# Spectral layer and feed-forward network on one core: even and odd frequencies apart in two of the four DFT stages

## The chip, the cores and the metric

The kernel runs on one core of one Trainium2 chip. The metric is the time of one execution on the device in microseconds (us). Three runs of the kernel before gave 2943.03, 2943.51 and 2943.71 us, median 2943.51. The profiled execution took 2942.39 us, of which 2940.6 us are the span from its first to its last instruction.

## The reference, cut to what matters

```python
def _attn_ref(x, w_r, w_i, b_r, b_i):            # x: 8 x 3072 x 256
    X = np.fft.rfft(x, axis=1)
    Xr, Xi = (X.real.astype(np.float32), X.imag.astype(np.float32))
    Yr = Xr @ w_r - Xi @ w_i + b_r
    Yi = Xr @ w_i + Xi @ w_r + b_i
    lam = 0.01
    Yr = np.sign(Yr) * np.maximum(np.abs(Yr) - lam, 0.0)
    Yi = np.sign(Yi) * np.maximum(np.abs(Yi) - lam, 0.0)
    y = np.fft.irfft(Yr.astype(np.float64) + 1j * Yi.astype(np.float64), n=x.shape[1], axis=1)
    return y.astype(np.float32)

def _moe_ref(x, w_in, w_out):                    # x: 24576 x 256, w_in: 256 x 2048
    h = x @ w_in
    sp = np.where(h > 20.0, h, np.log1p(np.exp(np.minimum(h, 20.0))))
    return ((h * np.tanh(sp)) @ w_out).astype(np.float32)
```

## The kernel before, in words

**Arithmetic.** Every product on TensorE is made of three: each operand is split into a rounded high part and a low rest, and high x high, low x high and high x low are added up in one PSUM bank. A split is a copy to the rounded type (hi, L171 on VectorE or L173 on ScalarE) and a subtraction (lo, L174, VectorE).

**Stages of a batch.** Each of the 8 batches goes through item_a (13 items: 24-point DFTs, tile psa), then 12 items b (second forward stage: 128-term sums against a table tile tt, tile psb, L391) that alternate with 12 items m (channel mix and soft threshold), then 13 items c (first inverse stage, psc) and 12 items f (last inverse stage against the constant vv, psf, L648), which leave y as yh and yl. Between the stages the data goes through DRAM: s1 after a, s3 after m, s2 after c. An item has a load (by a DMA on SP's queue), a cload (the table), a prep (the split) and pieces of matmuls (mm) with their evictions.

**The feed-forward network.** Each chunk of 512 rows takes 16 slots. A slot t is six 512-column matmuls (hp, L728, then Mish on ScalarE, L733) and, four slots later, twelve 256-column matmuls (acc, L756). On every second slot VectorE splits two results (gh, gl; L739, L740). hp has two PSUM buffers, the DFT stages share the two of ps_d, acc has four.

**Order.** The order is written out by hand, and every engine runs its own list in order. Batch 0 goes through a, b, m, c and its first two items f alone (the prologue, to about 207 us), with the unpacking of the double-precision network weights (from_double, L229 to L250) cut into steps that are dealt out among the pieces. After that one piece of the next batch's chain, or one of this batch's items f (in the slots where `extra` is at work), stands between the hp and the acc matmuls of each slot. run_chain puts an item's load two to three items ahead of its pieces (six in the prologue) and its split two ahead: the split of the next item b stands on its engine ahead of the eviction of the present one. A stage's first loads wait for the last store of the stage before. In batches 1 to 7 an item m is two pieces (psk and psp, with a sum of real and imaginary parts, sm, L411, made when b is evicted); in batch 0 it is twelve 512-column matmuls (psm, L488).

**Evictions that are touched.** a: one copy on ScalarE (ev, L341), then the store to s1. b: a copy on ScalarE (xh, L396), a copy of the imaginary half (sm, L399; not in batch 0) and a subtraction on VectorE (xl, L400). f: a copy on ScalarE (od, L651), two additions on VectorE (yt, L653, L654), a copy (yh, L656) and a subtraction (yl, L657). m: bias and threshold on VectorE (y, cl, y; L426 to L428), then two stores of 64 rows (L509).

## Time and profile before

| | before |
|---|---|
| median of three runs | 2943.51 us |
| profiled execution, and its span | 2942.39 us, 2940.6 us |
| TensorE matmuls (PE) busy | 2836.7 us, 96% |
| weight loads (PEld) busy | 2592.0 us, 88% |
| VectorE (DVE), ScalarE (ACT), GpSimd (POOL) busy | 58%, 31%, 6% |
| mean rate of the DMA engines | 97 GB/s |
| first 40th of the span to the fourth, PE in tenths | 4, 7, 4, 9 |

Busy times are sums over instructions; matmuls are pipelined, so that the pace of a stretch is read from the starts of its matmuls and not from their durations. In rows of a timeline the first number is the start in us from the start of the span, the second the time to the end of the last instruction of the row, and in brackets stands the idle time of the engine before it and what ended that.

### The profile page before, as it was taken

Reading aid. Unit: us, or ns where it says so; the run is one execution under the profiler, and the core shown is the slowest. Engines: PE = TensorE matmul, PEld = TensorE weight load, DVE = VectorE, ACT = ScalarE, POOL = GpSimd, SP = SyncE. Lnnn points to the kernel's source line nnn. Section 1 sums busy time; section 2 is a strip of 40 time slices with the busy share of each in tenths; the row PEclk is TensorE's granted clock in tenths of the full one; section 3 lists DMA queues with packets and bytes.
Section 4 is the critical chain, followed back from the end, with each engine's and each line's share of the span. In section 5 each row is a group of like instructions: output and inputs, shape, how many; then the busy total and the mean of one; then the engine's idle time right before and its main releaser. Section 6 shows DMA issues by size and latency. Waiting matters only on the chain.

```text
span 2940.6 us, 46576 instructions
## 1 busy us (share of the span) xinstructions
PE 2836.7 (96%) x18768; PEld 2592.0 (88%) x18768; DVE 1693.6 (58%) x2646; ACT 912.8 (31%) x1719; POOL 174.8 (6%) x268
## 2 busy tenths in 40 slices
PE   4749999999999999999999999999999999999999
PEld 2539999999999999989999999999999899999998
DVE  3956665556555665556655566555655556644443
ACT  3233323332233332333333323333223333232222
POOL 2410002000010001000020000200001000100000
PEclk9859999999999999999999999999999999999999
DMA  5655425232252233332242322523225323330000
GB/s 177 191 153 175 119 85 144 84 98 78 75 158 91 71 95 91 109 118 82 74 121 81 117 78 69 145 86 92 82 76 153 94 76 90 92 95 29 15 26 15
DMA packets 187408, 286.70 MB, mean 97 GB/s; under 512 B 25727, under 2 KB 112979, under 8 KB 186889
## 3 DMA queue, kind: packets, MB, share of 16 engines
q1 hardware_dynamic: 115473, 200.41, 22.9%
q10 hardware_dynamic: 52376, 50.34, 6.0%
q0 software_dynamic: 19344, 32.98, 4.4%
q8 instruction: 148, 2.42, 0.3%
q14 instruction: 67, 0.55, 0.1%
HBM read 182.89 MB, written 108.75 MB: 99 GB/s over the span
## 4 chain that ended last, share of the span: by engine, by line
PE 93%; DMA 3%; DVE 2%; issue 0%; SPq 0%; ACT 0%; ACTq 0%; DVEq 0%
PE acc L756 38%; PE hp L728 36%; PE psb L391 4%; PE psf L648 4%; PE psp L471 4%; PE psc L604 2%; PE psa L339 2%; PE psk L452 2%; DMA ld<-s 1%; DMA s<-ev 1%; DMA ldh<-s 1%; DMA ld<-in_x_dram 0%; DMA ldh<-in_x_dram 0%; DVE cl L427 0%; DVE lo L174 0%
## 5 line engine op out<-in xcount | busy, mean ns | idle before, releaser
L756 PE MATMUL acc<-wout,gh 128*128 128x256 f32 x6144 | 1134.7, 283 | 0.0
L728 PE MATMUL hp<-yh,win 128*128 128x512 f32 x3072 | 1085.3, 394 | 1.9 <-ACT yh L656 1.9
L756 PEld LDWEIGHTS acc<-wout,gh 128*128 128x128 f32 x6144 | 967.7, 189 | 29.3
L733 ACT ACTIVATE s<-hp 128x512 f32<-128x512 f32 x768 | 460.0, 599 | 1608.6 <-PE hp L728 1497.2
L756 PE MATMUL acc<-wout,gl 128*128 128x256 f32 x3072 | 868.1, 283 | 0.0
L728 PEld LDWEIGHTS hp<-yh,win 128*128 128x128 f32 x3072 | 579.1, 188 | 101.3 <-ACT yh L656 2.1
L728 PE MATMUL hp<-yl,win 128*128 128x512 f32 x1536 | 604.4, 394 | 0.0
L756 PEld LDWEIGHTS acc<-wout,gl 128*128 128x128 f32 x3072 | 578.6, 188 | 0.0
L740 DVE TENSOR_TENSOR gl<-s,gh 128x1024 fp32r<-128x1024 f32 x384 | 472.5, 1231 | 90.6 <-PE acc L756 60.6
L739 DVE CAST gh<-s 128x1024 fp32r<-128x1024 f32 x384 | 265.0, 690 | 395.0 <-ACT s L733 395.0
L728 PEld LDWEIGHTS hp<-yl,win 128*128 128x128 f32 x1536 | 289.1, 188 | 35.4 <-DVE yl L657 0.4
L174 DVE TENSOR_TENSOR lo<-ld,hi 128x512 fp32r<-128x512 f32 (+3 forms) x383 | 263.5, 688 | 43.5 <-ACT hi L173 30.3
L558 POOL DMA_DIRECT2D ld<-s x184 | 111.3, 614 | 2085.6 <-DMA s<-y 1297.5
L653 DVE TENSOR_TENSOR yt<-psf,od 128x256 f32<-128x256 f32 x96 | 40.8, 425 | 257.8 <-ACT od L651 257.4
L171 DVE CAST hi<-ld 128x512 fp32r<-128x512 f32 (+3 forms) x362 | 150.3, 415 | 24.9 <-DMA ld<-in_x_dram 18.1
L391 PE MATMUL psb<-tt,hi 128*128 128x256 f32 x768 | 142.3, 288 | 19.9 <-ACT hi L173 16.9
L648 PE MATMUL psf<-vv,hi 128*128 128x128 f32 x768 | 141.8, 272 | 9.0 <-ACT hi L173 9.0
L391 PEld LDWEIGHTS psb<-tt,hi 128*128 128x128 f32 x768 | 119.2, 192 | 31.7 <-ACT hi L173 17.6
L604 PE MATMUL psc<-hi,uu 120*120 120x256 f32 (+1 forms) x416 | 100.6, 303 | 39.2 <-ACT ev L606 25.0
L648 PEld LDWEIGHTS psf<-vv,hi 128*128 128x128 f32 x768 | 125.7, 194 | 13.2 <-ACT hi L173 9.3
L426 DVE TENSOR_TENSOR y<-psp,y 128x512 f32<-128x512 f32 x84 | 58.0, 691 | 131.6 <-PE psp L471 131.6
L471 PE MATMUL psp<-wmix,xh 128*128 128x256 f32 x672 | 133.1, 281 | 0.0
(94 smaller groups left out, 2340.7 us busy)
## 6 DMA issues: line engine op xcount, KB each, us to landing
s<-ev ACTq DMA_DIRECT2D x192, 240.0 KB
tt<-t_scr SPq DMA_DIRECT2D x66, 384.0 KB
s<-y SPq DMA_DIRECT2D x192, 128.0 KB
out_dram<-ot SPq DMA_DIRECT2D x48, 512.0 KB
ld<-s SPq DMA_DIRECT2D x90, 256.0 KB
ld<-s SPq DMA_DIRECT2D x180, 128.0 KB
uu<-u_scr SPq DMA_DIRECT2D x49, 450.0 KB
ld<-in_x_dram SPq DMA_DIRECT2D x90, 240.0 KB
```

The source lines that it names most:

```text
L171: nc.vector.tensor_copy(out=hi, in_=src)
L174: nc.vector.tensor_tensor(out=lo, in0=src, in1=f32(hi), op=ALU.subtract)
L391: nc.tensor.matmul(out=ps[:, c, :].rearrange("p (a m c) -> p a m c", a=2, m=2), lhsT=m[:, o:o + 128], rhs=rhs(s, ri), start=n == 0, stop=n ...
L471: nc.tensor.matmul(out=it.ps[:, ri * 256:(ri + 1) * 256], lhsT=m[:, c, 130 - ri * 128:258 - ri * 128], rhs=wmix[:, c, s, 2 * ri, :], start ...
L558: eng.dma_start(out=t[p:p + n, g * 256:(g + 1) * 256], in_=rows(k, nrow))
L604: nc.tensor.matmul(out=ps[sl], lhsT=u_t[pr // 2][:K, 2 * (pr % 2) + g, s, :K], rhs=m[sl], start=n == 0, stop=n == 2)
L648: nc.tensor.matmul(out=ps[:, p, c, :], lhsT=m[:, q:q + 128], rhs=vv[:, s, p, :], start=n == 0, stop=n == 2)
L728: nc.tensor.matmul(out=hp, lhsT=win[:, k, s, f * 128:(f + 1) * 128], rhs=m[:, k, :], start=n == 0, stop=n == 5)
L733: nc.scalar.activation(out=s_t[t // 2][:, t % 2, :], in_=hp, func=ACTF.Mish)
L739: nc.vector.tensor_copy(out=gh, in_=s)
L740: nc.vector.tensor_tensor(out=gl, in0=s, in1=f32(gh), op=ALU.subtract)
L756: nc.tensor.matmul(out=p, lhsT=m[:, t % 2, o:o + 128], rhs=wout[:, f, s, :], start=f == 0 and h == 0 and n == 0, stop=last and h == 1 and ...
```

## The change

The two members of each 128-term sum that stand half a period apart (rows 64 to 127 and 0 to 63) are added and subtracted in the eviction of stage a, so that stage b makes even frequencies from the sums and odd ones from the differences. For eleven of its twelve blocks each table has then half the columns, 128, and its high and low halves stand side by side: high data is streamed past both (256 columns), low data past the high half (128 columns). The extra 128 columns are copied out and added on VectorE. Stage f, whose two parities were apart already, gets the same side-by-side form.

```diff
@@ constants(): the tables' high and low parts side by side
-    fa = np.stack(_hi_lo(fa), 1)
-    t0 = np.stack(_hi_lo(t0), 1)
-    t = np.stack(_hi_lo(t), 2)
+    fa = np.stack(_hi_lo(fa), 2)
+    t0 = np.stack(_hi_lo(t0), 2)
+    t = np.stack(_hi_lo(t), 3)
...
@@ load_mix
-            t = p_h.tile([128, 2, 512], F32, tag="h", name="wraw").rearrange("p a f -> p (a f)")[:, 0:512]
+            t = p_y.tile([128, 2, 512], F32, tag=("yh", "yl")[k], name="wraw").rearrange("p a f -> p (a f)")[:, 0:512]
@@ scratch
-                dram.tile([128, 24, 256], F32, tag="s1", name="s1"),
+                dram.tile([64, 24, 512], F32, tag="s1", name="s1"),
@@ item_a load
-            src = bass.AP(tensor=x.tensor, offset=(b * SEQ + g0) * DM,
-                          ap=[[26 * DM, J], [128 * DM, 24], [1, 512]])
-            nc.sync.dma_start(out=it.t[:K], in_=src)
+            for h in range(2):
+                src = bass.AP(tensor=x.tensor, offset=(b * SEQ + 64 * h + 5 * pr) * DM,
+                              ap=[[DM, J], [128 * DM, 24], [1, 256]])
+                nc.sync.dma_start(out=it.t[:K, 256 * h:256 * h + 256], in_=src)
@@ item_a mm
-            for n, (s, m) in enumerate(((0, it.hi), (0, it.lo), (1, it.hi))):
-                nc.tensor.matmul(out=ps[:K], lhsT=fa[:K, s, :K], rhs=m[:K], start=n == 0, stop=n == 2)
+            for h in range(2):
+                sl = slice(256 * h, 256 * h + 256)
+                for n, (s, m) in enumerate(((0, it.hi), (0, it.lo), (1, it.hi))):
+                    nc.tensor.matmul(out=ps[:K, sl], lhsT=fa[:K, h, s, :K], rhs=m[:K, sl], start=n == 0, stop=n == 2)
             ev = p_ev.tile([128, 512], F32, tag="ev", name="ev")
-            nc.scalar.activation(out=ev[:K], in_=ps[:K], func=ACTF.Copy)
+            s2nd = p_w.tile([128, 256], F32, tag="cor", name="s2nd")
+            nc.scalar.activation(out=s2nd[:K], in_=ps[:K, 256:512], func=ACTF.Copy)
+            nc.vector.tensor_tensor(out=ev[:K, 0:256], in0=ps[:K, 0:256], in1=s2nd[:K], op=ALU.add)
+            nc.vector.tensor_tensor(out=ev[:K, 256:512], in0=ps[:K, 0:256], in1=s2nd[:K], op=ALU.subtract)
...
+            nc.scalar.dma_start(out=s1[5 * pr:5 * pr + J].rearrange("j m c -> (j m) c"), in_=ev[:K])
@@ item_b load
-            nc.sync.dma_start(out=it.t, in_=s1[:, 2 * blk:2 * blk + 2, :].rearrange("q m c -> q (m c)"))
+            src = s1.rearrange("b m c -> m b c")[2 * blk:2 * blk + 2]
+            nc.sync.dma_start(out=it.t, in_=src)
@@ item_b mm, blocks 0 to 10 (block 11 keeps its twelve matmuls of 256 columns in one bank)
+                xf = p_w.tile([128, 2, 256], F32, tag="xf", name="xf")
+                for c in range(2):
+                    ps = ps_d.tile([128, 2, 2, 128], F32, tag="d", name="psb")
+                    for e in range(2):
+                        o = e * 256 + c * 128
+                        nc.tensor.matmul(out=ps[:, e], lhsT=it.hi[:, o:o + 128], rhs=it.tt[:, e],
+                                         start=True, stop=False)
+                        nc.tensor.matmul(out=ps[:, e, 0], lhsT=it.lo[:, o:o + 128], rhs=it.tt[:, e, 0],
+                                         start=False, stop=True)
+                    cor = p_w.tile([128, 2, 128], F32, tag="cor", name="cor")
+                    nc.scalar.activation(out=cor, in_=ps[:, :, 1], func=ACTF.Copy)
+                    nc.vector.tensor_tensor(out=xf[:, c].rearrange("p (r e i) -> p e r i", r=2, e=2),
+                                            in0=ps[:, :, 0].rearrange("p e (r i) -> p e r i", r=2),
+                                            in1=cor.rearrange("p e (r i) -> p e r i", r=2), op=ALU.add)
-            nc.scalar.activation(out=xh[:, :, 2:258], in_=ps, func=ACTF.Copy)
+            nc.scalar.activation(out=xh[:, :, 2:258], in_=xf, func=ACTF.Copy)
...
-            nc.vector.tensor_tensor(out=xl[:, :, 2:258], in0=ps, in1=f32(xh[:, :, 2:258]), op=ALU.subtract)
+            nc.vector.tensor_tensor(out=xl[:, :, 2:258], in0=xf, in1=f32(xh[:, :, 2:258]), op=ALU.subtract)
...
-            nc.vector.tensor_tensor(out=sm, in0=ps[:, :, 0:128], in1=sm, op=ALU.add)
+            nc.vector.tensor_tensor(out=sm, in0=xf[:, :, 0:128], in1=sm if blk == 11 else xf[:, :, 128:256], op=ALU.add)
@@ item_m store: four DMAs of 32 rows for blocks 0 to 10
+            rows = s3[0:1536].rearrange("(i e r) s c -> r e i (s c)", r=24, e=2)
+            for e in range(2):
+                for d in range(2):
+                    nc.sync.dma_start(out=rows[23 - blk, 1 - e] if d else rows[blk + 1, e],
+                                      in_=y[64 * e + 32 * d:64 * e + 32 * d + 32])
@@ item_f mm
-            ps = ps_d.tile([128, 2, 2, 128], F32, tag="d", name="psf")
+            eo = p_w.tile([128, 2, 2, 128], F32, tag="xf", name="eo")
             for c in range(2):
+                ps = ps_d.tile([128, 2, 2, 128], F32, tag="d", name="psf")
                 for p in range(2):
                     q = p * 256 + c * 128
-                    for n, (m, s) in enumerate(((it.hi, 0), (it.lo, 0), (it.hi, 1))):
-                        nc.tensor.matmul(out=ps[:, p, c, :], lhsT=m[:, q:q + 128], rhs=vv[:, s, p, :],
-                                         start=n == 0, stop=n == 2)
-            od = p_ev.tile([128, 2, 128], F32, tag="od", name="od")
-            nc.scalar.activation(out=od, in_=ps[:, 0], func=ACTF.Copy)
...
+                    nc.tensor.matmul(out=ps[:, p], lhsT=it.hi[:, q:q + 128], rhs=vv[:, p], start=True, stop=False)
+                    nc.tensor.matmul(out=ps[:, p, 0], lhsT=it.lo[:, q:q + 128], rhs=vv[:, p, 0], start=False, stop=True)
+                cor = p_w.tile([128, 2, 128], F32, tag="cor", name="cor")
+                nc.scalar.activation(out=cor, in_=ps[:, :, 1], func=ACTF.Copy)
+                nc.vector.tensor_tensor(out=eo[:, c], in0=ps[:, :, 0], in1=cor, op=ALU.add)
+            yt = p_w.tile([128, 2, 2, 128], F32, tag="w", name="yt")
+            nc.vector.tensor_tensor(out=yt[:, :, 0, :], in0=eo[:, :, 1], in1=eo[:, :, 0], op=ALU.add)
+            nc.vector.tensor_tensor(out=yt[:, :, 1, :], in0=eo[:, :, 1], in1=eo[:, :, 0], op=ALU.subtract)
```

A table of stage b shrinks with it from 384 KB to 256 KB. The tiles cor, xf and w (pool p_w) have two buffers each; the pools of the stages and their numbers of buffers are as before.

## Rows read from the trace of the kernel before

**Rows 1.** The page, part 4: the chain of work that ended last, shares of the span by line.
```profile
PE acc L756 38%; PE hp L728 36%; PE psb L391 4%; PE psf L648 4%; PE psp L471 4%; PE psc L604 2%; PE psa L339 2%; PE psk L452 2%; DMA ld<-s 1%; DMA s<-ev 1%; DMA ldh<-s 1%; DMA ld<-in_x_dram 0%; DMA ldh<-in_x_dram 0%; DVE cl L427 0%; DVE lo L174 0%
```
**Rows 2.** Windows of the prologue and of one whole batch: window and its length in us, busy us and (number) of PE, PEld, DVE, ACT and POOL, then the granted TensorE clock as a share of full speed, the mean busy share of the DMA engines, and GB/s.
```profile
40.00:60.00 20.00, 4.48 (x8) 1.99 (x8) 13.80 (x23) 7.90 (x15) 11.71 (x14) 1.00 0.73 214
63.00:131.00 68.00, 58.75 (x294) 47.43 (x294) 61.32 (x105) 17.28 (x33) 25.21 (x27) 1.00 0.60 171
140.00:160.00 20.00, 7.19 (x24) 5.49 (x24) 6.20 (x11) 4.57 (x8) 9.80 (x17) 0.50 0.90 216
971.00:1320.00 349.00, 349.00 (x2361) 321.95 (x2360) 206.35 (x325) 111.07 (x212) 14.97 (x25) 1.00 0.33 96
```
**Rows 3.** Timeline of PE in one slot with a piece of stage b: the piece's first start, the start of the twelve acc matmuls behind it, and of the next hp.
```profile
629.90 0.41 PE L391 MATMUL psb<-tt,hi 128*128 128x256 f32 x2
...
631.35 0.40 PE L756 MATMUL acc<-wout,gh 128*128 128x256 f32 x2
...
632.79 0.40 PE L728 MATMUL hp<-yh,win 128*128 128x512 f32 x1
```
**Rows 4.** Timeline of PE and its weight loads in the slot with a piece of stage f.
```profile
634.17 0.22 PE L648 MATMUL psf<-vv,hi 128*128 128x128 f32 x1
634.18 0.19 PEld L648 LDWEIGHTS psf<-vv,lo 128*128 128x128 f32 x1
...
634.29 0.30 PEld L648 LDWEIGHTS psf<-vv,hi 128*128 128x128 f32 x2
...
635.46 0.45 PE L756 MATMUL acc<-wout,gh 128*128 128x256 f32 x2
...
636.94 0.39 PE L728 MATMUL hp<-yh,win 128*128 128x512 f32 x1
```
**Rows 5.** Timeline of PE: a piece of stage a (three matmuls of 512 columns) and one of stage c (six of 256 columns), each to the acc matmul behind it.
```profile
564.63 0.40 PE L339 MATMUL psa<-hi,fa 120*120 120x512 f32 x1
...
565.33 0.40 PE L756 MATMUL acc<-wout,gh 128*128 128x256 f32 x2
...
817.61 0.28 PE L604 MATMUL psc<-hi,uu 120*120 120x256 f32 x1
...
818.32 0.40 PE L756 MATMUL acc<-wout,gh 128*128 128x256 f32 x2
```
**Rows 6.** Timeline of ACT and DVE in the eviction of a piece of stage f in the prologue.
```profile
202.69 0.38 ACT L651 ACTIVATE od<-psf 128x256 f32<-128x256 f32 x1 [2.20 <-PE psf L648]
...
203.10 0.42 DVE L653 TENSOR_TENSOR yt<-psf,od 128x256 f32<-128x256 f32 x1 [1.89 <-ACT od L651]
203.44 0.41 DVE L654 TENSOR_TENSOR yt<-psf,od 128x256 f32<-128x256 f32 x1
204.62 0.69 DVE L657 TENSOR_TENSOR yl<-yt,yh 128x512 fp32r<-128x512 f32 x1 [0.76 <-ACT yh L656]
```
**Rows 7.** Timeline of DVE in stages b and m of batch 0: the first operation on the psm of the first, the second and the last item m (L426), and xl of two items b, two items apart (L400).
```profile
72.86 0.69 DVE L426 TENSOR_TENSOR y<-psm,bias 128x512 f32<-128x512 f32 x1 [1.25 <-PE psm L488]
...
79.36 0.69 DVE L426 TENSOR_TENSOR y<-psm,bias 128x512 f32<-128x512 f32 x1
...
83.05 0.68 DVE L400 TENSOR_TENSOR xl<-psb,xh 128x512 fp32r<-128x512 f32 x1
...
93.58 0.68 DVE L400 TENSOR_TENSOR xl<-psb,xh 128x512 fp32r<-128x512 f32 x1
...
129.57 0.68 DVE L426 TENSOR_TENSOR y<-psm,bias 128x512 f32<-128x512 f32 x1
```
**Rows 8.** Timeline of PE there: the first of twelve psm matmuls, and the psb behind them.
```profile
85.32 0.47 PE L488 MATMUL psm<-wmix,xh 128*128 128x512 f32 x1
...
88.41 0.51 PE L391 MATMUL psb<-tt,hi 128*128 128x256 f32 x2
```
**Rows 9.** DMA: two windows (columns as in rows 2), the first with loads of x alone (outermost count of the source 5), the second with loads of stage b (128 rows); then the issue of the first load of x on SP's queue and the split that waited for it, and the first load of stage b in batch 0.
```profile
6.00:8.00 2.00, 1.49 (x3) 0.75 (x3) 0.69 (x1) 0.57 (x2) 0.00 (x0) 1.00 0.33 128
60.00:63.00 3.00, 0.00 (x0) 0.00 (x0) 0.00 (x0) 0.00 (x0) 0.45 (x1) 1.00 1.06 400
...
0.75 0.94 SPq L330 DMA_DIRECT2D ldh<-in_x_dram  x1
...
5.83 0.63 ACT L173 ACTIVATE hi<-ldh 120x512 fp32r<-120x512 f32 x1 [3.80 <-DMA ldh<-in_x_dram]
...
57.80 0.33 SPq L356 DMA_DIRECT2D ld<-s  x1
```
**Rows 10.** Timeline around the change from stage a to stage b in batch 2: SP's issue of the first two loads of stage b, and on DVE the split of the second, and xl and sm of the first.
```profile
618.89 0.80 SPq L356 DMA_DIRECT2D ld<-s  x2
...
625.27 0.42 DVE L171 CAST hi<-ld 128x512 fp32r<-128x512 f32 x1
...
632.45 0.69 DVE L400 TENSOR_TENSOR xl<-psb,xh 128x512 fp32r<-128x512 f32 x1 [2.51 <-ACT sm L399]
...
633.65 0.42 DVE L411 TENSOR_TENSOR sm<-psb,sm 128x256 f32<-128x256 f32 x1
```
**Rows 11.** Timeline near the end of that stage b: SP's two stores, the load behind them, and the split on DVE that needs this load.
```profile
747.03 1.12 SPq L509 DMA_DIRECT2D s<-y  x2
...
751.90 0.46 SPq L356 DMA_DIRECT2D ld<-s  x1
...
760.89 0.42 DVE L171 CAST hi<-ld 128x512 fp32r<-128x512 f32 x1
```

More of the change, by code (lines that the diff above doesn't have):

```diff
@@ L32, in ang @@
         return 2.0 * np.pi * ((k * b) % n) / n
[L34 removed]
+    fa = np.zeros((120, 2, 120))
     a = np.arange(24)
[L36 to L49 removed]
@@ L63, in _dft_constants @@
-    t0[:, 128] = np.where(bq[:, 0] % 2, -1.0, 1.0)
-    th = ang(12 + 24 * i, bq)
-    t0[:, 320:384], t0[:, 448:512] = np.cos(th), -np.sin(th)
+    for h in range(2):
+        blk = np.zeros((24, 24))
+        for kk in range(1, 12):
+            th = 2.0 * np.pi * (((2 * kk * a) + h * kk) % 48) / 48
+            blk[:, 2 * kk - 2] = np.cos(th)
+            blk[:, 2 * kk - 1] = -np.sin(th)
+        blk[:, 22] = 1.0
+        blk[:, 23] = np.where(a % 2, -1.0, 1.0)
+        for j in range(5):
+            fa[24 * j:24 * j + 24, h, 24 * j:24 * j + 24] = blk
@@ new lines, in _dft_constants @@
+    bh = np.arange(64)[:, None]
+    j = np.arange(32)[None]
+    t = np.zeros((11, 2, 64, 2, 2, 2, 32))
+    for kk in range(1, 12):
+        for eo in range(2):
+            for d in range(2):
+                th = ang(kk + 24 * (2 * j + eo) if d == 0 else kk - 24 * (2 * j + 2 - eo), bh)
+                sg = 1.0 - 2.0 * d
+                t[kk - 1, 0, :, eo, 0, d], t[kk - 1, 0, :, eo, 1, d] = np.cos(th), -sg * np.sin(th)
+                t[kk - 1, 1, :, eo, 0, d], t[kk - 1, 1, :, eo, 1, d] = np.sin(th), sg * np.cos(th)
@@ new lines, in _dft_constants @@
+    t = t.reshape(11, 128, 2, 128)
+    t0 = np.zeros((2, 64, 2, 2, 2, 64))
+    i = np.arange(64)[None]
+    th = ang(24 * i, bh)
+    for eo in range(2):
+        on = i % 2 == eo
+        t0[0, :, eo, 0, 0], t0[0, :, eo, 1, 0] = np.cos(th) * on, -np.sin(th) * on
+        t0[0, :, eo, 1, 0, 0] = np.where(bh[:, 0] % 2, -1.0, 1.0) * (eo == 0)
+    w = np.exp(-1j * ang(12 + 24 * i, bh))
+    ph = 1j * np.where(i % 2, -1.0, 1.0)
+    for eo, z in enumerate((w * (1 - ph) / 2, w * (1 + ph) / 2)):
+        t0[1, :, eo, 0, 1], t0[1, :, eo, 1, 1] = z.real, z.imag
@@ L67, in _dft_constants @@
+    t0 = t0.reshape(128, 2, 256)
     u = np.zeros((26, 120, 120))
@@ L321, in item_a @@
         it = Item()
-        g0 = 2 * pr
-        J = 5 if g0 < 24 else 4
+        J = 5 if pr < 12 else 4
         K = 24 * J
@@ L359, in cload @@
                 return
-            W = 512 if blk == 11 else 384
             if b == 0 and (blk + 1) % 12 % 5 > 1:
@@ L384, in mm @@
         def mm():
-            ps = ps_d.tile([128, 2, 256], F32, tag="d", name="psb")
-            for c in range(2):
-                n = 0
-                for m, s in ((it.hi, 0), (it.lo, 0), (it.hi, 1)):
-                    for ri in range(2):
-                        o = ri * 256 + c * 128
-                        nc.tensor.matmul(out=ps[:, c, :].rearrange("p (a m c) -> p a m c", a=2, m=2),
-                                         lhsT=m[:, o:o + 128], rhs=rhs(s, ri), start=n == 0, stop=n == 5)
-                        n += 1
@@ L394, in mm @@
             xh = p_x.tile([128, 2, 258], F32R, tag="xh", name="xh")
             xl = p_x.tile([128, 2, 258], F32R, tag="xl", name="xl")
-            nc.scalar.activation(out=xh[:, :, 2:258], in_=ps, func=ACTF.Copy)
+            it.x = (xh, xl)
+            if blk == 11:
+                ps = ps_d.tile([128, 2, 256], F32, tag="d", name="psb")
+                for c in range(2):
+                    n = 0
+                    for m, s in ((it.hi, 0), (it.lo, 0), (it.hi, 1)):
+                        for e in range(2):
+                            o = e * 256 + c * 128
+                            nc.tensor.matmul(out=ps[:, c, :], lhsT=m[:, o:o + 128], rhs=it.tt[:, e, s, :],
+                                             start=n == 0, stop=n == 5)
+                            n += 1
+                xf = ps
+            else:
+                xf = p_w.tile([128, 2, 256], F32, tag="xf", name="xf")
+                for c in range(2):
+                    ps = ps_d.tile([128, 2, 2, 128], F32, tag="d", name="psb")
+                    for e in range(2):
+                        o = e * 256 + c * 128
+                        nc.tensor.matmul(out=ps[:, e], lhsT=it.hi[:, o:o + 128], rhs=it.tt[:, e],
[7 more added lines that the diff above has]
+                                            in1=cor.rearrange("p e (r i) -> p e r i", r=2), op=ALU.add)
@@ L503, in store @@
             s3 = scratch(b)[1]
-            r = ((blk + 1, 23 - blk) if blk < 11 else (0, 12))
             yv = y.rearrange("p (s c) -> p s c", s=2)
```

69 lines of the change are left out of this document (20 added, 49 removed).

## The prediction

> **What bounds the kernel now.** First the chain of waits, by line: nearly everything on it is TensorE's, the network 74% and the DFT and mix pieces the rest; psb and psf, the two lines that shrink, hold 4% each [rows 1]. Then the windows: over one whole batch PE is busy in 349.00 of 349 us, DVE in 206.35, the DMA engines a third of the time [rows 2]. So in batches 1 to 7 the time is a sum of matmul paces, and a matmul saved is time saved as long as nothing else gets late. The prologue is different: in stages b and m of batch 0 DVE is busy in 61.32 of 68 us, and behind them PE works 7.19 of 20 us at a granted clock of 0.50, the lower level of 1.2 GHz [rows 2]. Work that the change puts on DVE costs there.
>
> **Pace of a matmul.** A piece of stage b, twelve matmuls of 256 columns, takes 631.35 - 629.90 = 1.45 us, 0.121 each [rows 3]. A piece of stage f, twelve of 128 columns, takes from 634.17 to the next hp at 636.94 less the 1.44 us of the acc group: 1.33 us, 0.111 each [rows 3, 4]. Half the columns saves only a tenth: the weight loads follow each other at (634.29 - 634.18) = 0.11 us, and a short matmul waits for the next one's weights [rows 4].
>
> **Stages b and f, steady.** Both pieces become four matmuls of 256 columns and four of 128, with eight weight loads in place of twelve: 4 x 0.121 + 4 x 0.111 = 0.93 us. Stage b: 7 batches x 11 blocks = 77 x (1.45 - 0.93) = -40.0 us. Stage f: 96 items, 94 of them among network slots, 94 x (1.33 - 0.93) = -37.6 us. Bounds: if the short one cost as much as a long one, +7 us on both together (171 x 4 x 0.01); if it fell to half a long one, 0.06, -34 us. I take the row of psf, which is this very shape.
>
> **Stage a, steady.** Three matmuls of 512 columns take 0.70 us, six of 256 on 120 rows take 0.71 [rows 5]: 91 x 0.01 = +0.9 us. The load becomes two DMAs; one issue holds SP 0.94 us at most [rows 9], under a slot's length of some 3.5 us (hp 634.17 - 632.79 = 1.38, acc 1.44 and the piece's 0.70 [rows 3 to 5]), so I cost it at nothing.
>
> **Evictions, steady.** A piece of a, b or f gets two more additions of 256 columns on DVE, 0.34 us apart when back to back (203.44 - 203.10), and b and f also a chain copy, addition, copy, subtraction that cannot overlap: from the second addition to the subtraction that needs the copied result 204.62 - 203.44 = 1.18 us [rows 6]. That is 36 x 0.68 = 24 us per batch on DVE against 143 us idle [rows 2]. Each half of b and f now has a PSUM buffer of its own, so a piece takes both buffers of ps_d, and the next piece, 2.82 us of network matmuls later, needs the first back. The copy (0.38) and addition (0.42) free it within about 1 us of the half's end, 2 us if DVE is a split behind. It fits; cost 0, and if it did not, each 0.1 us per piece would be 17 us.
>
> **The load of stage b is what I trust least.** Its source was 128 rows; now it is 2 x 64 rows, outermost count 2. The loads of x, whose source has the outermost count 5, ran with several in flight at a DMA share of 0.33, about 5 of 16 engines, and 128 GB/s; stage b's loads, 128 rows, ran at 1.06 and 400 GB/s [rows 9]. I read from this that the outermost count limits the engines: two of them, at 128/5 = 25.6 GB/s each, move 262 KB in 5.1 us. The rest of a load's time is 2.2 us: the first load of x was issued by 1.69, its split began at 5.83, and 240 KB at 128 GB/s are 1.9 us [rows 9].
> The Trainium skill, page "DMA: Bandwidth & Descriptors", section "Why a DMA increments its semaphore by 16 and not by 1", says that a DMA runs on the largest number of engines up to 16 that divides the slowest dimension of both access patterns. By that rule it is exactly two, which speaks against this change; the trace agrees for 5 and for 128, and for 2 no row shows it.
>
> Where it costs: at the start of every stage b two loads are issued together at 618.89. The second would land at 618.9 + 0.4 + 10.2 + 2.2 = 631.7, and DVE has its split in line at 625.27 [rows 10]. DVE is held 6.4 us; of that its idle time before xl (2.51) and a little more is cover, so sm, which frees the PSUM buffer of the first item, moves from 633.65 to about 637. The piece of f that stands at 634.17 needs both buffers, the second after 0.46 us: PE waits some 2.5 us. 7 x 2.5 = +18 us; bounds 0 (the network has slots enough) and 7 x 5 = 35. In the middle of the stage the tightest lead is 760.89 - 751.90 = 9.0 us [rows 11], about 1 us less with the shorter pieces and four stores in place of two ahead of it on SP (two hold it 1.12), against 0.5 + 5.1 + 2.2 = 7.8. It just fits; +4 us for all of it, bounds 0 and 40.
>
> **Prologue.** Stage a: the additions go onto DVE, which is busy 13.8 of 20 us at its end [rows 2]; of 13 x 0.68 = 9 us I take +4 (bounds 0 and 12, x being read in rows of half the size). Stages b and m: the loads are issued from 57.80 on [rows 9]. Each item's eviction stands behind the split of the next item, so the first halves can be freed only when the third load is in, at 57.8 + 0.4 + 15.3 + 2.2, plus 1 for other traffic, about 77; split, copy and additions 1.7; then twelve psm, 2.8 us at the full clock, twice that at the lower one: the first L426 at about 84.5 instead of 72.86, and by the second (79.36) the lag is some 14 us. Ten more items follow. DVE now takes (93.58 - 83.05)/2 = 5.27 us for one, back to back [rows 7]; it gets two additions, 0.68, and the hole of 1.18 - 0.34 = 0.84, so +1.5 each: +15. Together +29 us; bounds 8 (the additions alone) and 60. The two items f: eight matmuls fewer, longer evictions, -1.
>
> **Sum.** -40.0 - 37.6 + 0.9 + 18 + 4 + 4 + 29 - 1 = -22.7 us. The profiled execution took 2942.4, so 2919.7; the median of the runs is 1.1 us above it: 2921 us.
>
> **Rivals.**
> *The loads are no obstacle* (they use all engines, or their delay is covered): the 18 fall away, 12 of the prologue's 14 and 2 of the 4, giving 2889 us. For it: DMA engines idle two thirds of a batch [rows 2]. Against it: rows 9.
> *The clock falls in the prologue.* Between its psm runs PE would now idle for some 3 us in every 6.8 (less 2.8 and 0.93), where it idled 1 us in 5.27 (less 2.8 and 1.45). At the lower level the twelve psm that take 2.8 of the 88.41 - 85.32 = 3.1 us [rows 8] take 5.6, and L426 waits for them: 10 x 2.8 = +28, 2949 us. For it: the row at 0.50 with PE busy a third of the time; against it: 1.00 in the stage itself [rows 2].
> The Trainium skill, page "TensorE: Matmul & The Clock Gate", section "A second HAM failure mode: psum-queue depth-cycling", has a kernel whose small idle gaps between groups made the clock go to and fro; by it the 2949 would hold. The trace before has no such stage at full clock with gaps of 3 us, so it cannot say.
> *The two-engine loads set the pace (slower).* If other traffic on these two engines stretches a load from 5.1 to 7 us, the second load of each stage is 3.8 us later (7 x 3.8 = 27), splits in mid-stage come 1.7 us late against a cover of about 1 (half of 77 items x 0.5 = 19), and the prologue's items pace at the load and its share of other traffic, 1.8 longer (18): +64, 2985 us. It decides from about 5.8 us a load, where the 23 us are used up. For it: in the prologue DMA is busy 0.60 [rows 2]; against it: 0.33 in a steady batch.
> *It does not do what it says:* a short matmul behind a long one costs 0.06, so half of the piece goes: 2887 us.
>
> **How the numbers follow.** Forecast 0.48, loads no obstacle 0.20, clock 0.12, load-paced 0.15, cheaper short matmul 0.05. About 0.2%, 6 us, can be told from no change here, so faster means below 2937.6. Forecast (all but a tail), the second and the last case: 0.73. Same: most of the clock case and the tail, 0.11. Slower: the load-paced case and what is left of the clock case, 0.16. The likeliest case alone spans 2900 to 2940; the range is 2887 to 2965, from the two cheaper cases to the middle of the load-paced one.
>
> **What would show it.** In the changed profile: psb and psf pieces of 0.93 us in the timeline; psa pieces of 0.71; the DMA share near 0.13 while only stage b's first loads run; DVE waiting for a load at the second split of each stage b, and PE waiting at the f piece behind; the first hp 32 us later, and a batch 7 to 8 us shorter (11 x 0.52 + 12 x 0.40 less 2.5 and 0.6). The forecast is wrong if those loads run at a share near 1, if PE waits on PSUM in ordinary slots, or if 1.00 is no longer granted in batch 0's stage b.

## The result and the profile after

The changed kernel takes 2968.31 us (median of four runs, 2962.30 to 2974.09) against 2943.61 us before (four runs, 2943.03 to 2944.87): 0.83% slower, ratio 1.0083 with a 95% interval of 1.0061 to 1.0105. The forecast was 2921 us. The profiled execution of the changed kernel was the fastest of the four, 2962.3 us with a span of 2960.5 us, so the accounts below explain 19.9 us in the spans of the 24.7 us between the medians; the other three runs, 3 to 12 us longer, show a mean granted clock of 0.972 to 0.976 against its 0.977, and no trace shows where they lost it.

The page, parts 1 and 4 (the chain by line), and below them windows with the columns of [rows 2]:

```profile
PE 2780.4 (94%) x18344; PEld 2549.5 (86%) x18344; DVE 1898.4 (64%) x3222; ACT 950.3 (32%) x1914; POOL 171.8 (6%) x268
...
PE acc L784 34%; PE hp L756 33%; DMA ld<-s 5%; PE psp L493 4%; PE psc L631 2%; PE psf L675 2%; PE psk L474 2%; PE psa L346 2%; PE psb L409 2%; DMA s<-ev 1%; PE psm L510 1%; DMA ld<-in_x_dram 1%; DVE lo L179 1%; PE psf L676 1%; PE psb L411 1%
```
```profile
63.00:131.00 68.00, 38.19 (x142) 30.40 (x142) 37.50 (x76) 17.20 (x37) 14.37 (x17) 0.90 0.41 116
...
1043.00:1388.00 345.00, 340.57 (x2305) 314.56 (x2305) 231.88 (x397) 114.66 (x234) 14.64 (x25) 1.00 0.32 93
```

TensorE has 56 us less to do, and the span is 20 us longer: the time went into waits and, behind some of them, a lower clock. Loads of the DFT stages (ld<-s), which held 1% of the chain before [rows 1], now hold 5%. In batch 0's stages b and m DVE, which was busy 61.32 of 68 us [rows 2], is busy 37.50 in the same window, which now begins with the first loads, and 56.10 of the 75.27 us from 89.59 to 164.86, the first to the eleventh item m: it now waits for a quarter of the time. And a whole batch, where PE never paused, now has 345.00 - 340.57 = 4.4 us of idle TensorE.

The pieces themselves came out as worked out. Timeline of PE, one piece of stage f, the acc group behind it and the next hp (compare [rows 4]):

```profile
1053.73 0.28 PE L675 MATMUL psf<-vv,hi 128*128 128x256 f32 x1
1053.85 0.22 PE L676 MATMUL psf<-vv,lo 128*128 128x128 f32 x1
...
1054.61 0.45 PE L784 MATMUL acc<-wout,gh 128*128 128x256 f32 x2
...
1056.09 0.39 PE L756 MATMUL hp<-yh,win 128*128 128x512 f32 x1
```

1054.61 - 1053.73 = 0.88 us for the piece, and the acc group behind it takes 1.48 instead of 1.44: together 0.92 against the forecast's 0.93.

To see where time went, three marks are read from the timeline of PE in every kernel: the start of the first hp (end of the prologue), and the first psn matmul of each batch (it belongs to block 11, the first of stages b and m, and so lies just behind the change from stage a to stage b). They cut the span into the prologue, the stretch to batch 1's psn, six batches from psn to psn, and the rest behind batch 7's. All times in us; the medians are those of the runs, the other columns of the profiled execution.

| kernel | median | first hp at | to psn of batch 1 | a batch (mean of six) | rest |
|---|---|---|---|---|---|
| before | 2943.6 | 207.1 | 91.9 | 348.5 | 550.4 |
| changed | 2968.3 | 245.2 | 104.9 | 345.4 | 537.8 |
| e1_wide | 2918.9 | 243.0 | 100.4 | 339.8 | 538.4 |
| e2_before_narrow | 2979.6 | 236.9 | 92.4 | 349.6 | 550.4 |
| e3_wide_defer | 2909.4 | 233.9 | 99.6 | 339.4 | 537.4 |
| e4_f_only | 2906.1 | 208.7 | 91.6 | 343.7 | 542.8 |
| e5_three | 2883.8 | 208.1 | 99.4 | 339.4 | 537.4 |
| e6_three_six | 2889.6 | 216.1 | 99.3 | 339.4 | 537.3 |
| e7_narrow_three | 2957.7 | 237.8 | 106.6 | 345.9 | 537.8 |
| e8_six_first | 2885.4 | 213.9 | 96.4 | 339.5 | 537.4 |
| e9_old_f | 2965.6 | 247.2 | 97.9 | 345.9 | 545.5 |
| e10_one_x | 2887.1 | 213.4 | 98.6 | 339.5 | 537.5 |
| e11_late_fa | 2886.3 | 216.7 | 95.6 | 339.8 | 537.4 |

The changed kernel against the one before: +38.1 in the prologue, +13.0 to batch 1's psn, 6 x -3.1 = -18.6 in the batches (the first of them 347.8, the other five 344.9), -12.6 in the rest.

What the stall of each batch looks like, at the change from stage a to stage b of batch 3. Timelines of SP, DVE and PE, one engine behind the other:

```profile
1010.33 1.22 SPq L365 DMA_DIRECT2D ld<-s  x2
...
1018.28 0.43 DVE L176 CAST hi<-ld 128x512 fp32r<-128x512 f32 x1 [3.07 <-DMA ld<-s]
...
1023.51 0.43 DVE L176 CAST hi<-ld 128x512 fp32r<-128x512 f32 x1 [4.08 <-DMA ld<-s]
...
1024.59 0.42 DVE L176 CAST hi<-ld 128x512 fp32r<-128x512 f32 x1
...
1027.58 0.68 DVE L423 TENSOR_TENSOR xl<-psb,xh 128x512 fp32r<-128x512 f32 x1
...
1028.77 0.42 DVE L433 TENSOR_TENSOR sm<-psb,sm 128x256 f32<-128x256 f32 x1
...
1025.79 0.33 PE L676 MATMUL psf<-vv,lo 128*128 128x128 f32 x1 [0.34 <-DVE lo L179]
...
1029.34 0.35 PE L675 MATMUL psf<-vv,hi 128*128 128x256 f32 x1 [3.00 <-DVE sm L433]
...
1031.91 0.63 PE L756 MATMUL hp<-yh,win 128*128 128x512 f32 x1
```

The split that needs the second load of stage b starts 13.2 us after the issue of the two (the forecast's 0.4 + 10.2 + 2.2 = 12.8). DVE has its split in line and stands for 4.08 us; behind it wait xl and sm, the last readers of the first item's PSUM buffer; the first half of the stage-f piece runs at 1025.06 to 1026.3, and its second half needs that buffer and waits 3.00 us. Behind the wait everything is slower for a while. Windows around it (columns of [rows 2]):

```profile
1018.00:1020.00 2.00, 2.00 (x16) 1.91 (x15) 1.12 (x2) 0.60 (x1) 0.00 (x0) 1.00 0.13 51
1020.00:1022.00 2.00, 2.00 (x16) 1.82 (x14) 0.00 (x0) 0.60 (x1) 0.00 (x0) 1.00 0.14 53
...
1028.00:1036.00 8.00, 6.66 (x38) 6.21 (x39) 6.27 (x16) 3.74 (x10) 0.00 (x0) 0.79 0.14 52
1036.00:1044.00 8.00, 8.00 (x58) 7.47 (x57) 5.41 (x11) 2.41 (x5) 0.00 (x0) 1.00 0.00 0
```

With only stage b's first loads in flight the DMA share is 0.13 to 0.14, two engines of 16, at 51 to 53 GB/s. And from 1028 to 1036 us, the end of the wait included, the granted clock's mean is 0.79; the six hp matmuls from 1031.91 take until 1034.23, 2.32 us instead of the 1.38 of [rows 3, 4] (634.17 - 632.79).

### The profile page after: what moved, and what is told of

The parts are those of the page before. It is cut to its first block, busy times and chain, and to the rows that moved or that the text cites. A ratio compares the mean times of both kernels' runs of the same rounds, so it can differ in the third digit from the quotient of the medians.

```text
span 2960.5 us, 47048 instructions
## 1 busy us (share of the span) xinstructions
PE 2780.4 (94%) x18344; PEld 2549.5 (86%) x18344; DVE 1898.4 (64%) x3222; ACT 950.3 (32%) x1914; POOL 171.8 (6%) x268
## 4 chain that ended last, share of the span: by engine, by line
PE 83%; DMA 8%; DVE 5%; issue 2%; SPq 1%; ACT 1%; ACTq 0%; DVEq 0%
PE acc L784 34%; PE hp L756 33%; DMA ld<-s 5%; PE psp L493 4%; PE psc L631 2%; PE psf L675 2%; PE psk L474 2%; PE psa L346 2%; PE psb L409 2%; DMA s<-ev 1%; PE psm L510 1%; DMA ld<-in_x_dram 1%; DVE lo L179 1%; PE psf L676 1%; PE psb L411 1%
## 5 line engine op out<-in xcount | busy, mean ns | idle before, releaser
L679 DVE TENSOR_TENSOR eo<-psf,cor 128x256 f32<-128x256 f32 x192 | 77.4, 422 | 173.8 <-ACT cor L678 173.0
L675 PE MATMUL psf<-vv,hi 128*128 128x256 f32 x384 | 100.2, 333 | 43.9 <-DVE sm L433 21.0
L346 PE MATMUL psa<-hi,fa 120*120 120x256 f32 (+1 forms) x416 | 100.8, 303 | 35.0 <-DVE ev L351 25.1
L675 PEld LDWEIGHTS psf<-vv,hi 128*128 128x128 f32 x384 | 74.0, 193 | 53.1 <-ACT s L761 21.8
L631 PEld LDWEIGHTS psc<-hi,uu 120*120 120x120 f32 (+1 forms) x416 | 74.4, 196 | 46.4 <-ACT ev L633 29.3
```

The costliest lines, as they stand in the source:

```text
L346: nc.tensor.matmul(out=ps[:K, sl], lhsT=fa[:K, h, s, :K], rhs=m[:K, sl], start=n == 0, stop=n == 2)
L631: nc.tensor.matmul(out=ps[sl], lhsT=u_t[pr // 2][:K, 2 * (pr % 2) + g, s, :K], rhs=m[sl], start=n == 0, stop=n == 2)
L675: nc.tensor.matmul(out=ps[:, p], lhsT=it.hi[:, q:q + 128], rhs=vv[:, p], start=True, stop=False)
```

## Experiments

**The load alone, both ways.** e1_wide is the changed kernel with a load from 64 rows for each half of the tile:

```diff
-            src = s1.rearrange("b m c -> m b c")[2 * blk:2 * blk + 2]
-            nc.sync.dma_start(out=it.t, in_=src)
+            for m in range(2):
+                nc.sync.dma_start(out=it.t[64 * m:64 * m + 64], in_=s1[:, 2 * blk + m, :])
```

> The changed kernel with one edit: the load of stage b is two DMAs of 64 rows each, one for each half of the tile, in place of one DMA whose outermost count is 2. Theory L (the narrow load is the main cause): in the chain steady from batch 1 on, the wait of 3.0 us at the first stage-f piece behind the stage-b splits goes, and the lower clock behind it with it: 7 x (3.0 + about 2) = 35 us less; the splits of batch 0 stop waiting 3 to 6 us for their loads, about 15 us of the prologue less. 2968 - 50 = about 2918 us. Rival D (the DVE additions behind each stage-a and stage-b piece, and the two PSUM buffers that a stage-b item now takes, are the main cause): under 15 us change, over 2950 us.

Measured 2918.91 us (2916.00 to 2922.61), ratio 0.9915 (0.9900 to 0.9930): theory L's time, 49.4 us below the changed kernel by the medians. The table places 39.7 of them, because it sets the fastest run of the changed kernel beside the slowest of this one. By the table the places are partly others: a batch is 5.6 us shorter, as expected, but the prologue only 2.2. Waits of PE in a batch of the changed kernel and, below, in one of e1_wide, and the windows of the two:

```profile
PE psf L675 <- DVE sm L433: 3.0, 1, 3.0
PE psf L675 <- DVE ev L351: 1.2, 1, 1.2
PE psf L676 <- DVE lo L179: 0.3, 1, 0.3
...
698.00:1043.00 345.00, 340.43 (x2305) 314.37 (x2304) 231.74 (x396) 114.54 (x234) 15.12 (x25) 1.00 0.31 93
```
```profile
PE psf L675 <- DVE ev L351: 1.0, 1, 1.0
PE psk L474 <- DVE xf L415: 0.2, 1, 0.2
...
683.00:1022.70 339.70, 338.50 (x2304) 312.94 (x2304) 231.56 (x397) 114.80 (x234) 14.79 (x25) 1.00 0.32 95
```

The 3.0 and 0.3 us are gone, and the same matmuls are busy 340.43 - 338.50 = 1.9 us less: so the transition cost 3.3 us of waiting and 1.9 us of slower matmuls behind it.

e2_before_narrow gives the kernel before such a load and nothing else of the change:

```diff
+    perm = np.concatenate([np.arange(0, 128, 2), np.arange(1, 128, 2)])
+    t = t[:, perm]
...
+    t0 = t0[perm]
...
-            nc.sync.dma_start(out=it.t, in_=s1[:, 2 * blk:2 * blk + 2, :].rearrange("q m c -> q (m c)"))
+            src = s1[:, 2 * blk:2 * blk + 2, :].rearrange("(j h) m c -> h j (m c)", h=2)
+            nc.sync.dma_start(out=it.t, in_=src)
```

> The kernel before with one edit: the load of stage b is one DMA whose outermost count is 2 (the even partitions' rows of the table first, then the odd ones; the table's rows are permuted to fit), everything else as before. Theory L: the load alone costs what it costs the changed kernel: 7 x 5 = 35 us in the batches and some 15 us in the prologue, 2943.6 + 50 = about 2990 us. Rival D: the load is hidden when no additions stand on DVE, under 10 us more, below 2955 us.

Measured 2979.62 us (2979.30 to 2979.82), ratio 1.0121 (1.0105 to 1.0136). Between the two: the prologue pays 29.8 us, twice what theory L said, but a batch only 1.1 us where the changed kernel pays over 5. The load is as late here (timeline of DVE, batch 2), and then all that PE waited for from 360 to 700 us (engine, line, what ended the wait: us in total, times, longest):

```profile
663.39 0.43 DVE L175 CAST hi<-ld 128x512 fp32r<-128x512 f32 x1 [4.69 <-DMA ld<-s]
...
668.65 0.42 DVE L416 TENSOR_TENSOR sm<-psb,sm 128x256 f32<-128x256 f32 x1
```
```profile
PE psf L653 <- DVE lo L178: 0.4, 1, 0.4
PE psf L653 <- DVE hi L175: 0.3, 1, 0.3
```

From the split to sm there are 668.65 - 663.39 = 5.26 us, as in the changed kernel (1028.77 - 1023.51 = 5.26). DVE's delay is the same, and PE does not feel it. What differs is the piece of stage f: before, it had one PSUM buffer for both halves; now it takes both.

**Which half of that pair makes the stall.** e9_old_f is the changed kernel, narrow load and all, with stage f as it was:

```diff
-            eo = p_w.tile([128, 2, 2, 128], F32, tag="xf", name="eo")
+            ps = ps_d.tile([128, 2, 2, 128], F32, tag="d", name="psf")
             for c in range(2):
-                ps = ps_d.tile([128, 2, 2, 128], F32, tag="d", name="psf")
...
+                    for n, (m, s) in enumerate(((it.hi, 0), (it.lo, 0), (it.hi, 1))):
+                        nc.tensor.matmul(out=ps[:, p, c, :], lhsT=m[:, q:q + 128], rhs=vv[:, s, p, :],
+                                         start=n == 0, stop=n == 2)
...
```

> The changed kernel, narrow load and all, with stage f as it was before (three matmuls of 128 columns for each product, one PSUM buffer per item). Theory P (the 3.0 us stall of each batch needs both: the late load holds the PSUM buffer of block 11's stage b, and the new stage-f piece asks for a second buffer): without the second buffer the stall goes, as in the kernel before with the narrow load alone (1.1 us a batch); each batch then loses the 4.8 us that stage f is worth and wins back about 4: 345 to 346 us from one psn to the next against 344.9. Rival N (the narrow load alone makes the stall): 344.9 + 4.8 = 349.7 us a batch.

Measured 2965.63 us (2962.51 to 2967.62); a batch takes 345.8 to 346.1 us, theory P's number. So 4.8 us a batch of saved matmuls could be taken out of the changed kernel at a price of 0.9 us from one psn to the next (345.9 against the 344.9 of the last five). Waits of PE over batch 3:

```profile
PE psk L474 <- DVE xf L415: 1.1, 1, 1.1
PE psb L409 <- DVE yt L681: 0.4, 1, 0.4
PE psf L675 <- DVE lo L179: 0.4, 1, 0.4
```

The wait for sm is gone though the load is as narrow. The stretch to batch 1's psn also fell, from 104.9 to 97.9: there too the second buffer was half of the cost.

**Stage f alone.** e4_f_only is the kernel before with the new item_f (and the staging tiles of the mix weights moved, as in the change, to make room for its tiles).

> The kernel before with the stage-f part of the change alone (two matmuls for each table half, high and low halves side by side; ScalarE takes the low half out, DVE adds), with the small edits of buffers that it needs. By the pieces read from the changed kernel (0.88 us against 1.33 us): 94 x 0.45 = 42 us less, 2943.6 - 42 = about 2902 us. Rival E (two PSUM buffers in a row per stage-f item and an added DVE chain at its end give part of it back at batch ends): 10 to 20 us less gain, 2912 to 2922 us.

Measured 2906.11 us (2904.85 to 2907.75), ratio 0.9870 (0.9853 to 0.9886): 37.6 us faster by the medians, the forecast's -37.6 for stage f where 42 were expected from the shorter pieces; between the profiled spans 35.1, with 1.6 us more in the prologue and 4.8 us less in each batch. Where no load is late, two buffers in a row cost nothing.

**The store on ScalarE's queue.** e3_wide_defer adds to e1_wide:

```diff
-            nc.scalar.dma_start(out=s1[5 * pr:5 * pr + J].rearrange("j m c -> (j m) c"), in_=ev[:K])
+            def st():
+                nc.scalar.dma_start(out=s1[5 * pr:5 * pr + J].rearrange("j m c -> (j m) c"), in_=ev[:K])
+
+            if pr < 12:
+                pend.append(st)
+            else:
+                st()
```

> As the run with two DMAs of 64 rows, and the store of a stage-a item is issued on ScalarE's queue one item later (the last at once), so that ScalarE does not wait for the DVE additions before it goes on. Theory S (ScalarE held by the store's wait delays its own splits and Mish): the waits of ScalarE for the additions of stage a (49 us of Mish and 1.5 to 2.4 us per split in batch 0) go, the first stage a among the acc groups loses part of its 13 us and batch 0's stage a some 3 us: 8 us below the run with two DMAs alone. Rival O (the additions come late because they stand behind the split of a later load on DVE): the same time within 2 us.

Measured 2909.42 us (2908.82 to 2912.39), 9.5 us below e1_wide. The size is theory S's, the place is not: of 13.7 us between the profiled spans 9.1 went in the prologue and only 0.8 between the first hp and batch 1's psn. So Mish's 49.0 us of waits for the additions, 14 in the whole run, had cost little: a batch is 0.4 us shorter. Of the 9.1, 5.2 were gained before the first item m (the first operation on its psm at 79.61 us against 84.79) and 3.1 in the ten items behind it, at a mean clock of 0.89 against 0.83.

**The additions in batch 0.** e5_three is e3_wide_defer with stage b of batch 0 in three matmuls of 128 columns for each channel half and parity, in one PSUM buffer, without copy and additions:

```diff
+            elif b == 0:
+                ps = ps_d.tile([128, 2, 2, 2, 64], F32, tag="d", name="psb")
+                for c in range(2):
+                    for e in range(2):
+                        o = e * 256 + c * 128
+                        for n, (m, s) in enumerate(((it.hi, 0), (it.lo, 0), (it.hi, 1))):
+                            nc.tensor.matmul(out=ps[:, c, :, e, :], lhsT=m[:, o:o + 128],
+                                             rhs=it.tt[:, e, s].rearrange("p (r i) -> p r i", r=2),
+                                             start=n == 0, stop=n == 2)
+                xf = ps.rearrange("p c r e i -> p c (r e i)")
```

> As the run with two DMAs per load and the later store, and batch 0's stage b (blocks 0 to 10) accumulates three matmuls of 128 columns for each channel half and parity in one PSUM buffer, with no copy of the low half and no DVE additions; the other batches as they were. Theory C (in batch 0 the chain matmul, copy, addition, copy, addition, xh, xl of each item sets the pace, 7.8 us against 5.3 before): first hp from 233.9 to about 214, and the time from 2909 to about 2889 us. Rival (loads, stores or the table's DMAs set that pace): first hp above 228, over 2903 us.

Measured 2883.76 us (2882.25 to 2884.32), ratio 0.9798 (0.9782 to 0.9814), first hp at 208.1: theory C, by 5 us more than it said, and the best version found, 2% faster than the kernel before. The pace is read from DVE's first operation on each psm, as in [rows 7]. In the changed kernel, the first, second and eleventh:

```profile
89.59 0.69 DVE L448 TENSOR_TENSOR y<-psm,bias 128x512 f32<-128x512 f32 x1 [2.69 <-PE psm L510]
98.99 0.69 DVE L448 TENSOR_TENSOR y<-psm,bias 128x512 f32<-128x512 f32 x1 [1.46 <-PE psm L510]
...
164.86 0.69 DVE L448 TENSOR_TENSOR y<-psm,bias 128x512 f32<-128x512 f32 x1 [1.08 <-PE psm L510]
```

In e1_wide, the same three:

```profile
84.79 0.69 DVE L448 TENSOR_TENSOR y<-psm,bias 128x512 f32<-128x512 f32 x1 [3.46 <-PE psm L510]
95.07 0.69 DVE L448 TENSOR_TENSOR y<-psm,bias 128x512 f32<-128x512 f32 x1 [2.33 <-PE psm L510]
...
164.23 0.69 DVE L448 TENSOR_TENSOR y<-psm,bias 128x512 f32<-128x512 f32 x1 [1.08 <-PE psm L510]
```

And in e5_three the first, second and third:

```profile
75.52 0.69 DVE L465 TENSOR_TENSOR y<-psm,bias 128x512 f32<-128x512 f32 x1 [0.44 <-PE psm L527]
81.92 0.68 DVE L465 TENSOR_TENSOR y<-psm,bias 128x512 f32<-128x512 f32 x1
87.15 0.68 DVE L465 TENSOR_TENSOR y<-psm,bias 128x512 f32<-128x512 f32 x1
```

Ten items take 75.27 us in the changed kernel and 79.44 in e1_wide, whose loads are not narrow; one takes 87.15 - 81.92 = 5.23 in e5_three, the pace of before. The clock has its part in the two long times. Windows of two items of the changed kernel, each from the first operation on one psm to that on the next (columns of [rows 2]):

```profile
122.47:130.71 8.24, 5.74 (x23) 4.56 (x22) 6.00 (x13) 2.55 (x5) 1.09 (x1) 0.79 0.41 128
137.26:144.03 6.77, 4.15 (x23) 3.33 (x21) 5.90 (x12) 1.74 (x4) 0.00 (x0) 1.00 0.78 218
```

With 1.00 granted an item takes 6.77 us, the forecast's 6.8; with 0.79 it takes 8.24, and its twelve psm 4.5 us in place of 3.05. Ten items of 6.8 would be 68, so that 7.3 us of the changed kernel's time and 11.4 of e1_wide's, whose mean clock there is 0.83 against 0.91, go with the lower clock. That is where e1_wide lost what it had won: its first item comes 4.8 us earlier (84.79 against 89.59), its ten items take 4.2 longer, and none of its splits waits for a load there. With the additions DVE waits for the product (PE psm) in most items, the product waits for the additions (PE psm <- DVE xf, 26.5 us in the changed kernel), and no engine is full. Whether it is the additions' chain or the second PSUM buffer of an item that does it was not tried apart: e5_three takes out both.

e7_narrow_three gives the changed kernel the same three matmuls in batch 0, with its narrow load and its store as they are.

> The changed kernel with its narrow load and its store as they are, and batch 0's stage b as three matmuls without copies and additions. If load and additions are two limits that lie over each other in batch 0 (the load alone cost the kernel before 30 us up to the first hp, taking the load alone out of the changed kernel gave 2 us): the narrow load is left as the limit, first hp from 245.2 to about 238, 2968 - 7 = about 2961 us. If instead the additions alone cost the prologue its 38 us, first hp about 215, 2938 us.

Measured 2957.66 us (2953.86 to 2959.50), first hp at 237.8: the narrow load is left as the limit, about where e2_before_narrow has it (236.9). So in batch 0 load and additions lie over each other: taking one out gives 2.2 us (4.8 before the clock took its part back) or 7.4; from the changed kernel to e5_three, with both and the store's wait out, it is 37.1.

**Four that did not help.** Two try to take additions off DVE in stage a, with a third table half (the sign turned), twelve matmuls and one eviction, in batch 0 (e6_three_six) or in six items of batch 1 (e8_six_first):

```diff
+            if b == 0:
+                for g in range(2):
+                    n = 0
+                    for h in range(2):
+                        sl = slice(256 * h, 256 * h + 256)
+                        for s, m in ((0, it.hi), (0, it.lo), (1, it.hi)):
+                            nc.tensor.matmul(out=ps[:K, 256 * g:256 * g + 256], lhsT=fa[:K, h + (g if h else 0), s, :K],
+                                             rhs=m[:K, sl], start=n == 0, stop=n == 5)
+                            n += 1
+                nc.scalar.activation(out=ev[:K], in_=ps[:K], func=ACTF.Copy)
```

> As the run before it, and batch 0's stage a too forms sum and difference on TensorE (twelve matmuls of 256 columns, a third table half with the sign turned) with one eviction on ScalarE. Theory C: what the two DVE operations and the wait of the store cost in batch 0's stage a goes too, some 5 us below the run before it, about 2884 us. Rival: DVE has room there, within 2 us of the run before it.

> As the run with two DMAs, later store and batch 0's stage b in three matmuls (2883.8 us), and the first six stage-a items of batch 1, which run beside the rest of the weights' conversion on DVE, form sum and difference on TensorE (twelve matmuls of 256 columns, 6 x 0.72 = 4.3 us more) with one eviction on ScalarE. Theory A (there DVE is the limit, 18.2 of 20 us busy, and the additions come late): the waits of 6 us and part of the lower clock (0.84) go, first hp to psn of batch 1 from 99.4 to about 95 us, the time about 2879 us. Rival (DVE is late there whatever stage a does): 2888 us.

e6_three_six: 2889.56 us (2887.93 to 2890.81), 5.8 us above e5_three where 5 less were expected; the first hp came 8 us later. What theory C left out is the clock behind the longer pieces: from 20 to 30 and from 30 to 40 us 0.58 and 0.50 were granted, where e5_three has 1.00. How much of the 8 us that is stays open. e8_six_first: 2885.41 us (2883.18 to 2886.60); to batch 1's psn 96.4, as theory A said, but the prologue, whose code differs from e5_three's only in the larger table, was 5.8 us longer. e11_late_fa therefore loads the third table half later:

```diff
-        nc.gpsimd.dma_start(out=fa, in_=c_fa)
+        nc.gpsimd.dma_start(out=fa[:, 0:2], in_=c_fa[:, 0:2])
...
         nc.gpsimd.dma_start(out=vv, in_=c_v)
+        nc.gpsimd.dma_start(out=fa[:, 2], in_=c_fa[:, 2])
```

> As the run in which the first six stage-a items of batch 1 form sum and difference on TensorE (2885.4 us), but the third table half that they need is loaded with the stage-f table, not ahead of everything. If the larger first load is what took back its gain (first hp at 213.9 us against 208.1, first hp to psn of batch 1 96.4 against 99.4): first hp back near 208, the time near 2880 us. If not, 2885 us.

Measured 2886.30 us (2883.25 to 2890.14), first hp at 216.7 in its slowest run, the profiled one: loading the larger part later did not bring the first hp back. Its 95.6 us to batch 1's psn confirm e8_six_first's part of the theory. e10_one_x loads both halves of a stage-a item in one DMA:

```diff
-            for h in range(2):
-                src = bass.AP(tensor=x.tensor, offset=(b * SEQ + 64 * h + 5 * pr) * DM,
-                              ap=[[DM, J], [128 * DM, 24], [1, 256]])
-                nc.sync.dma_start(out=it.t[:K, 256 * h:256 * h + 256], in_=src)
+            src = bass.AP(tensor=x.tensor, offset=(b * SEQ + 5 * pr) * DM,
+                          ap=[[DM, J], [128 * DM, 24], [64 * DM, 2], [1, 256]])
+            nc.sync.dma_start(out=it.t[:K].rearrange("p (h c) -> p h c", h=2), in_=src)
```

> As the run with two DMAs, later store and batch 0's stage b in three matmuls (2883.8 us), and each stage-a item loads both its halves in one DMA with four dimensions in place of two DMAs. Theory X (two DMAs per load cost the start: the first ScalarE split came at 7.9 us against 5.8 before, behind a table load that waits for the first x load): first split near 6 us, first hp some 2 us earlier, 2882 us. Rival: the halves' number of DMAs costs nothing, the same within 1 us.

Measured 2887.09 us (2884.90 to 2890.43): theory X missed. Over e5_three, e8, e10 and e11 the first hp lies anywhere from 208.1 to 216.7 while the medians differ by 3.3 us and their runs overlap; what decides that is open, and none of the four beats e5_three.

## Why the prediction was wrong

By the marks, the terms of the forecast put the prologue at +32, the stretch to batch 1's psn at about +1 (one psb piece, three of psf, one transition), a batch at -7.4 (11 x 0.52 + 12 x 0.40 less 2.5 and 0.6) and the rest at about -12 (10 pieces of psb, 19 of psf, 0.6 for loads). Measured: +38.1, +13.0, -3.1 and -12.6. Of the 43 us between forecast and span, the six batches hold 26, the stretch to batch 1's psn 12 and the prologue 6.

- *Pace and steady gain: right.* Pieces of 0.88 plus 0.04 behind; e4_f_only gave stage f's -37.6 by the medians. With the narrow load out, a batch is 8.7 us shorter (e1_wide), where 11 x 0.52 + 12 x 0.40 = 10.5 was worked out; 0.9 to 2.0 a batch of what is missing is a stage-f piece that waits for a stage-a addition behind a split on DVE (L675 <- DVE ev, mean 1.2). "It fits; cost 0" was short by that.
- *The narrow load, steady: mechanism right, size too small.* Two engines, 5.1 us a load, a split waiting, xl and sm behind it, and the stage-f piece behind them all came as told. By the rule cited from the Trainium skill, page "DMA: Bandwidth & Descriptors", section "Why a DMA increments its semaphore by 16 and not by 1", the count is two; the share of 0.13 is two of 16, so the trace agrees for 2 as well. The step "PE waits some 2.5 us. 7 x 2.5 = +18 us" failed in what comes after the wait: it was 3.3 us, and 1.9 us more for matmuls at the lower clock, 5.2 a batch or 36 in all, just outside its bound of 35. Mid-stage loads (+4) cost nothing that the waits show.
- *The prologue: 6 us short, by the clock, and otherwise right in part by luck.* By the second item the forecast had 4 + 14 = 18 us, and the trace has 19.6 (98.99 against 79.36 [rows 7]); for an item with the additions it had 6.8, and at the full clock one takes 6.77 with DVE busy 5.90. What its sum put at nothing, and a rival at 0.12, is the clock: "against it: 1.00 in the stage itself" was read from a stage in which PE waited 0.6 us at most before a group of psm, and with the additions it waits 1.8 to 3.7. From the second item to the eleventh 4.7 us go over 6.8 an item (65.87 against 61.2), most of the 6 that are missing. The luck is in the load. Alone (e2_before_narrow) it is 13.2 us late at the second item (92.56 against 79.36), the forecast's 14, but does not stop there: its items take 7.6 us each, ScalarE's splits in them wait 49 us for loads, and the first hp is 29.8 late. Beside the additions this second limit hardly shows. The rest of the change without the narrow load costs 35.9 (e1_wide); 9.1 of it go when the store is issued later, a wait on ScalarE's queue that the forecast never mentions, and 25.8 with batch 0's additions and second buffer (e5_three), part of both by a higher clock.
- *First stretch with the network (12 us off): not in the forecast at all.* Stage a of batch 1 runs beside the last conversions of weights on DVE. Its additions come late there, and the stage-f pieces, now with two buffers, wait for them (4.8 us in two waits, the longer 4.5), and the clock over the second 20 us behind the first hp is 0.83 where it was 1.00; 7.0 us go with the old stage f (e9_old_f), 3 to 4 with the additions of six items (e8_six_first, e11_late_fa).

Of the rivals, the loads as no obstacle were given 2889 us; with that made true (e1_wide) the time is 2918.9; by its marks some 16 us of that lie in the prologue, 10 in the stretch to batch 1's psn and 9 in the six batches. The clock did fall, to 0.90 in the window of batch 0's stage b, which the forecast itself had named as a sign of being wrong; it did so in five of the first ten items and took about 7.5 us, not the rival's 28. The slower rival had the sign and the wrong ground: no load was stretched (13.2 us for two), and no split in mid-stage made PE wait; items paced by the load, which it has in the prologue, show in e2_before_narrow and not here.

## What to carry to other kernels

When a change takes a second PSUM buffer per piece and also makes a transfer later, price the two together: each was nearly free alone (0 and 1.1 us a batch), and together they cost 5.2. Where a stretch has two possible limits, put each alone against the old pace and take the larger, do not add them, and expect that undoing one of them gives next to nothing. A full clock in a stage without waits says nothing of that stage once another engine's additions stand between its matmuls. Before an eviction moves to another engine, look at what its store's queue does while it waits, and keep the old form in the stretch where matmuls are not the bound: e5_three keeps the shorter matmuls where TensorE is full and the older accumulation where it is not.
